# Turning the last two row tiles of a block by DMA instead of on TensorE, with two projections reordered, in a 32-head attention and SwiGLU kernel

## The chip, the cores and the metric

The kernel runs on one core of a Trainium2 chip. The metric is the time of one execution on the device, in microseconds (us); lower is better. All runs here are "fast": none is over 1.5% above the fastest of its kernel.

"PE" is TensorE (matmul), "PEld" its weight load, "DVE" VectorE, "ACT" ScalarE, "POOL" GpSimd, and "SP" or "SPq" the engine and queue that issue the DMAs followed here. "L410" is line 410 of the kernel. Times in the text count from the span's start.

## The reference

```python
# x: 1 x 2048 x 640; 32 heads, k and v caches 32 x 2048 x 192; all bf16
xn = layernorm(x)
q  = (xn @ wq) split into 32 heads of 192
s  = softmax(q @ k^T * 192**-0.5) @ v, heads joined, @ wo
g  = silu((silu(xn @ w1) * (xn @ w3)) @ w2)      # 640 -> 1536 -> 640
out = x + s * g
```

## The kernel before

x's 2048 rows are four blocks of 512 (`qb`), each of four row tiles of 128. Every projection needs the normalised block transposed (`xnT`: 640 features on partitions, rows along the free axis). A tile can be turned in two ways:

```python
def ln_turn(g, i2, copy):            # two tiles, on PE: ten 128x128 transposes into PSUM, then one copy
    pst = ps_st.tile([P, 2, DC, P], BF16, tag="st2", name="pst")
    for k in range(2):
        xn = xns.pop((g, 2 * i2 + k))
        for c in range(DC):
            nc.tensor.transpose(out=pst[:, k, c, :], in_=xn[:, c*P:(c+1)*P], identity=ident_bf[:])
    copy(out=xnT[...], in_=pst[:])

def ln_turn_dma(g, i):               # one tile, by a DMA transpose on the SP queue
    nc.sync.dma_start_transpose(out=xnT[:, :, q0:q0 + P], in_=xns.pop((g, i))[:])
```

`swap_halves(g)` then makes, with two DMAs, a copy `xnS` of the block with its partition halves exchanged; heads 1 to 31 need both. The work is a stream of steps. Step `n` of head `h` and block `qb` handles 256 keys (`p` counts them, eight steps to a block). `scores` is six matmuls into a PSUM tile of tag `st2`, then an exponential on ACT; `values` is sixteen matmuls. Scores run two steps ahead of values, and `st2` has two buffers, which projections and PE transposes share.

```python
for n, (h, qb, p) in enumerate(stream):
    if p == 0 and n > 0:
        project(h + 1, qb) ...       # next head's q of this block: 20 matmuls on xnT and xnS
    if h == 0 and qb == 0 and p == 3:
        project(1, 0)                # head 1's first projection
    if h == 0 and qb + 1 < NQB and p == (5 if qb == 0 else 4):
        project0(qb + 1)             # first head's q of the next block: 10 matmuls on xnT,
                                     # then casts (DVE, ACT) and three q copies (DVE)
    scores(n + 2)
    values(n)
    ...
    if h == 0:
        first_head(qb, p)            # layer norm of the blocks to come, on DVE, inside these steps
```

## Time and profile before

| | before |
|---|---|
| median of the first three runs | 1939.36 us (1938.64 to 1939.67) |
| profiled span | 1936.7 us |
| PE busy | 1927.1 us |
| granted clock | 1.0 |

From the page of the kernel before: the span, the busy time of PE, and the shares of the chain of work that ended last.

```profile
span 1936.7 us, 59668 instructions
PE 1927.1 (100%) x27273; PEld 1317.2 (68%) x27281; DVE 654.4 (34%) x997; ACT 1181.5 (61%) x1278; POOL 282.1 (15%) x501
PE 99%; DVE 0%; DMA 0%; ACT 0%; issue 0%
```

PE is busy for nearly the whole span, and it is also the chain that ended last. So the time is PE's work plus any hole in it, and an edit counts only if it takes PE work away or opens or closes a hole.

Next, a piece of that chain in order of time, before (start us, length us, what).

```profile
19.57 2.16 PE ps L424 x20
...
22.38 0.67 PE obank L516 x16
23.05 0.66 PE pst L354 x10
23.71 0.32 PE st L487
...
24.46 0.67 PE obank L516 x16
25.13 0.32 PE ps L410
...
25.50 1.89 PE ps L410 x8
27.39 0.32 PE st L487
```

Each piece starts where the last one ends. 19.57 is `project(1, 0)`, 23.05 the ten transposes, 25.13 `project0(1)`. The period from one value group to the next is 2.08 us across the transposes (22.38 to 24.46); an ordinary step takes 1.31.

The timeline of the same stretch, the normalisation of the two tiles, the SP queue and the copy that ends the PE turn (start us, busy us, engine, line, what, out<-in, count, idle time before and its releaser).

```profile
18.28 2.64 SPq L360 DMA_TRANSPOSE xnT<-xn  x2
...
20.66 0.80 DVE L346 TENSOR_SCALAR xn<-x_all,mv,rstd 128x640 bf16<-128x640 bf16 x2 [0.81 <-POOL rstd L327]
...
20.97 0.57 SPq L214 DMA_DIRECT2D x_all<-in_A_x_dram  x1
...
23.75 0.82 DVE L356 COPY xnT<-pst 128x1280 bf16<-128x1280 bf16 x1 [0.25 <-PE pst L354]
...
24.97 0.63 SPq L364 DMA_DIRECT2D xnS<-xnT  x1
```

The SP queue turns tiles 0 and 1 of block 1, then loads x's last block (640 KB, landed at 26.53), then swaps the halves of block 1 once the PE turn is copied out.

### The profile page before, as it was taken

Reading aid. Unit: us, or ns where it says so; the run is one execution under the profiler, and the core shown is the slowest. Engines: PE = TensorE matmul, PEld = TensorE weight load, DVE = VectorE, ACT = ScalarE, POOL = GpSimd, SP = SyncE. Lnnn points to the kernel's source line nnn. Section 1 sums busy time; section 2 is a strip of 40 time slices with the busy share of each in tenths; the row PEclk is TensorE's granted clock in tenths of the full one; section 3 lists DMA queues with packets and bytes.
Section 4 is the critical chain, followed back from the end, with each engine's and each line's share of the span. In section 5 each row is a group of like instructions: output and inputs, shape, how many; then the busy total and the mean of one; then the engine's idle time right before and its main releaser. Section 6 shows DMA issues by size and latency. Waiting matters only on the chain.

```text
span 1936.7 us, 59668 instructions
## 1 busy us (share of the span) xinstructions
PE 1927.1 (100%) x27273; PEld 1317.2 (68%) x27281; DVE 654.4 (34%) x997; ACT 1181.5 (61%) x1278; POOL 282.1 (15%) x501
## 2 busy tenths in 40 slices
PE   9999999999999999999999999999999999999998
PEld 6666666666666666666666666666666666577776
DVE  7333333333333333333333333333333334521111
ACT  6677676767676767776777777677767677210000
POOL 3111111111111111111111111111111110000000
PEclk9999999999999999999999999999999999999999
DMA  8643433323333434363434343434334220937772
GB/s 181 129 101 67 98 68 85 84 59 92 58 90 61 99 64 97 68 162 68 101 66 100 69 101 69 101 64 100 69 68 97 60 67 2 249 79 137 152 153 60
DMA packets 394643, 178.98 MB, mean 92 GB/s; under 512 B 341616, under 2 KB 382832, under 8 KB 394384
## 3 DMA queue, kind: packets, MB, share of 16 engines
q1 hardware_dynamic: 371136, 125.32, 31.5%
q0 software_dynamic: 19472, 45.71, 10.1%
q8 instruction: 215, 3.52, 0.8%
q10 hardware_dynamic: 3776, 4.06, 0.6%
q14 instruction: 44, 0.36, 0.1%
HBM read 52.82 MB, written 27.79 MB: 42 GB/s over the span
## 4 chain that ended last, share of the span: by engine, by line
PE 99%; DVE 0%; DMA 0%; ACT 0%; issue 0%
PE obank L516 35%; PE st L487 34%; PE ps L424 14%; PE ps_s L111 11%; PE ps_f L728 3%; PE ps_gu L702 1%; PE st L488 1%; PE ps L410 0%; DMA x_all<-in_A_x_dram 0%; DVE stats L316 0%; PE ps L391 0%; PE pst L354 0%; PE pk L271 0%; ACT pT L490 0%; DVE mv L317 0%
## 5 line engine op out<-in xcount | busy, mean ns | idle before, releaser
L490 ACT ACTIVATE pT<-st 128x1024 bf16<-128x1024 f32 x1024 | 1047.4, 1023 | 248.8 <-PE st L488 233.2
L516 PEld LDWEIGHTS <-pT 64*128 64x128 bf16 x16384 | 711.6, 94 | 242.0 <-ACT pT L490 0.2
L516 PE MATMUL obank<-vt,pT 64*128 64x193 bf16 x16384 | 849.6, 243 | 0.0
L487 PE MATMUL st<-qC,KW 64*128 64x512 bf16 x2046 | 605.6, 376 | 0.1
L525 DVE COPY osum<-obank 128x772 f32<-128x772 f32 x128 | 123.1, 962 | 786.9 <-PE obank L516 786.9
L488 PE MATMUL st<-qB,KW 64*128 64x512 bf16 x1024 | 385.0, 376 | 0.0
L487 PE MATMUL st<-qA,KW 64*128 64x512 bf16 x1022 | 384.3, 376 | 0.3 <-ACT pT L490 0.3
L488 PE MATMUL st<-qC,KW 64*128 64x512 bf16 x1022 | 384.3, 376 | 0.0
L488 PE MATMUL st<-qA,KW 64*128 64x512 bf16 x1022 | 384.3, 376 | 0.0
L487 PEld LDWEIGHTS <-KW 64*128 64x128 bf16 x3068 | 278.4, 94 | 153.3 <-issue 2.1
L424 PE MATMUL ps<-xnT,W 64*128 64x512 bf16 x1280 | 297.3, 376 | 0.0
L424 PE MATMUL ps<-xnS,W 64*128 64x512 bf16 x1280 | 296.2, 376 | 0.0
L488 PEld LDWEIGHTS <-KW 64*128 64x128 bf16 x3068 | 278.5, 94 | 0.8 <-issue 0.6
L377 POOL DMA_DIRECT2D qC<-qA x124 | 65.4, 528 | 1283.4 <-DVE rl_all L532 1268.5
L430 ACT CAST qB<-ps 128x512 bf16<-128x512 f32 x131 | 76.8, 586 | 228.2 <-PE ps L424 222.7
L111 PE MATMUL ps_s<-wo_sb,oT 128*128 128x384 bf16 (+3 forms) x1535 | 208.7, 299 | 0.1
L424 PEld LDWEIGHTS <-W 64*128 64x128 bf16 x2560 | 123.6, 94 | 120.7
L111 PEld LDWEIGHTS <-oT 128*128 128x128 bf16 x1536 | 148.4, 98 | 60.4
L526 DVE TENSOR_TENSOR osum<-osum,obank 128x772 f32<-128x772 f32 x128 | 122.7, 959 | 13.4
L533 DVE TENSOR_TENSOR ostage<-osum,rl_all 128x768 bf16<-128x768 f32 x128 | 122.6, 958 | 6.2 <-DMA o_scr<-ostage 1.9
L465 DVE SCALAR_TENSOR_TENSOR hT<-pt,qB 64x512 bf16<-64x512 bf16 x64 | 43.8, 684 | 197.6 <-ACT pt L464 197.6
L429 DVE CAST qA<-ps 128x512 bf16<-128x512 f32 x131 | 90.6, 692 | 25.3 <-PE ps L410 7.2
(84 smaller groups left out, 620.8 us busy)
## 6 DMA issues: line engine op xcount, KB each, us to landing
o_scr<-ostage SPq DMA_DIRECT2D x16, 1536.0 KB, 10.6
vt<-in_A_v_cache_dram SPq DMA_DIRECT2D x63, 384.0 KB, 5.9
qC<-qA POOLq DMA_DIRECT2D x248, 64.0 KB, 2.0
qC<-qB POOLq DMA_DIRECT2D x124, 64.0 KB, 2.3
wo_sb<-in_A_wo_dram POOLq DMA_DIRECT2D x1, 7680.0 KB, 37.8
W<-in_A_wq_dram POOLq DMA_DIRECT2D x32, 160.0 KB, 3.6
W<-in_B_w_dram POOLq DMA_DIRECT2D x32, 80.0 KB, 3.3
W<-in_A_wq_dram POOLq DMA_DIRECT2D x32, 80.0 KB, 2.9
```

The source lines that it names most:

```text
L111: nc.tensor.matmul(ps[:, 0:w], lhsT=oT[:, k, :], rhs=wo_sb[:, k, c0:c1], start=(k == 0), stop=(k == OC - 1))
L377: nc.gpsimd.dma_start(out=qC[0:64, half, :], in_=qAB[half][64:P, :])
L424: nc.tensor.matmul(ps[:, r * 512:(r + 1) * 512], lhsT=W[rows, j, :], rhs=xs[rows, j // 2, qs], start=(j == 0), stop=(j == 2 * DC - 1))
L429: a = nc.vector.tensor_copy(out=qAB[0][:], in_=ps[:, 0:512])
L430: b = nc.scalar.copy(out=qAB[1][:], in_=ps[:, 512:1024])
L487: nc.tensor.matmul(st2[:, 0:512], lhsT=ka, rhs=qa, start=r == 0 and nr == 3, stop=r == nr - 1)
L488: nc.tensor.matmul(st2[:, 512:1024], lhsT=kb, rhs=qb2, start=r == 0 and nr == 3, stop=r == nr - 1)
L490: nc.scalar.activation(out=pT2[:], in_=st2[:], func=ACT.Exp, scale=att_scale)
L516: nc.tensor.matmul(obanks[r][:, j * 256:j * 256 + DH + 1], lhsT=pT2[r * 64:(r + 1) * 64, t * 512 + j * P:t * 512 + (j + 1) * P], rhs=vt[r ...
L525: nc.vector.tensor_copy(out=osum[:], in_=ov[0])
L526: nc.vector.tensor_tensor(out=osum[:], in0=osum[:], in1=ov[1], op=ALU.add)
L533: nc.vector.tensor_tensor(out=ostage[:, qb * 4:qb * 4 + 4, hg * DH:(hg + 1) * DH], in0=osum[:, :, 0:DH], in1=rl.unsqueeze(2).to_broadcast( ...
```

## The change

The intent: take the last transposes off PE, give the DMAs one more step to land, and put head 1's first projection behind the first-head projection, so that PE has work while the new q is copied.

```diff
     def first_head(qb, p):
         if qb == 0 and p == 1:
-            ln_norm(1, 2, nc.vector)
-            ln_norm(1, 3, nc.vector)
+            for i in (2, 3):
+                ln_norm(1, i, nc.vector)
+                ln_turn_dma(1, i)
+            swap_halves(1)
         if qb == 0 and p == 3:
             ln_stats(2, 0)
-            ln_turn(1, 1, nc.vector.tensor_copy)
-            swap_halves(1)
@@ the loop over steps
-        if h == 0 and qb == 0 and p == 3:
+        if h == 0 and qb + 1 < NQB and p == (6 if qb == 0 else 4):
+            project0(qb + 1)
+        if h == 0 and qb == 0 and p == 6:
             project(1, 0)
-        if h == 0 and qb + 1 < NQB and p == (5 if qb == 0 else 4):
-            project0(qb + 1)
```

## The prediction

> **What bounds the kernel now.** TensorE: the page gives PE 1927.1 us busy of 1936.7 (100%), and the chain that ended last is 99% PE. From 15 us on, the chain of waits has no hole. A step of head 0 (scores 0.65 us of the chain, values 0.67) repeats every 1.31 us. So only PE work taken away, or a new hole in PE's stream, can matter. The change touches only the first 40 us.
>
> **What it removes.** Ten PE transposes of the last two row tiles of x's block 1: 0.66 us of the chain (23.05 to 23.71), and the score matmul behind them takes 0.32 instead of 0.21. The period between value groups is 2.08 us there (22.38 to 24.46), not 1.31: 0.77 us comes off the critical path. Their VectorE copy (0.82 us) goes too, off the path.
>
> **What it moves.** Head 1's first projection (2.16 us, at 19.57) goes behind block 1's first-head projection (2.2 us, at 25.13), itself a step later. This is neutral in PE work, and hides the q copies (1.5 us of VectorE, 27.44 to 28.96) that the next scores need.
>
> **What it adds.** Two DMA transposes, on which the first-head projection waits directly; it needs all 512 columns. Before, a projection and the transposes stood ahead of it on PE. Now three plain steps follow 19.57, so PE arrives at 19.57 + 3 x 1.31 = 23.5 us, earlier than the 25.1 of before although "a step later".
>
> VectorE ends the tiles' normalisation at 21.46. The SP queue first issues the load of x's last block (20.97 to 21.54), then the two transposes (1.2 to 1.3 us of issue each): at 21.6 and 22.9. The DMA view gives 2.6 to 5.1 us from issue to landing for such transposes, so the second lands at 25.5 at the earliest. The load ahead (640 KB) landed at 26.5. [...] So I expect landing near 27.7 (26 to 29.5). Estimated hole in PE: 27.7 - 23.5 = 4.2 us.
>
> **Balance.** +4.2 - 0.77 = +3.4 us. A possible extra: the granted clock fell to half 3.2 us after this trace's last matmul and rose 3.6 us after its first. If the hole trips this, some 3.5 us of matmuls run at half speed, +1.8 us; I give it one chance in three. Head 1's projection of block 1 follows the landing by about 7 us, and the half swap that it needs took 5.7 us from its issue: no second hole, narrowly.
>
> Predicted: 1943.0 us, 8 in 10 between 1940.3 and 1946.6: +0.2% on 1939.36. Faster by over 2%: 0.005; within 2%: 0.985; slower by over 2%: 0.01. Slower by any amount: 0.92.
>
> **What would show it.** In the timeline: no transposes near 23 us; three steps straight after 19.57; PE idle from 23.5 to about 27.7, released by the DMA of xnT, then the two projections back to back; later steps shifted by about 3.4 us with equal periods; PE clock below 1 near 26 to 31 us if the clock falls.
>
> **What would make it wrong.** Transposes that overtake the load (hole about 2 us, total +1.2); the clock falling, or a late half swap (+2 more); or transposes that land before 24 us: then 0.8 us faster.

## The result, and the profile after

| | before | after |
|---|---|---|
| median of six runs | 1938.84 us (1938.13 to 1939.67) | 1944.88 us (1943.27 to 1945.15) |
| profiled span | 1936.7 us | 1943.1 us |
| mean granted clock, profiled run | 1.0 | 0.998 |

The ratio is 1.0029 (95% interval 1.0016 to 1.0042): slower by 0.3%, the same by a margin of 2%. Ratios are the mean time of one kernel's fast runs over that of the other's of the same rounds, so they are not quite the ratios of the medians quoted here.

The page after, the same three lines:

```profile
span 1943.1 us, 59651 instructions
PE 1928.0 (99%) x27263; PEld 1315.4 (68%) x27271; DVE 653.6 (34%) x996; ACT 1180.2 (61%) x1278; POOL 282.4 (15%) x501
PE 98%; DMA 1%; DVE 0%; ACT 0%; SPq 0%; issue 0%
```

PE's busy time hardly moved (0.9 us more), but the span grew by 6.4, and a DMA now stands in the chain. The chain in order of time shows where:

```profile
22.84 5.72 DMA xnT<-xn
28.55 0.14 issue
28.69 0.58 PE ps L410
...
29.50 3.59 PE ps L410 x8
33.09 2.27 PE ps L424 x20
```

The second new transpose was issued at 22.84 and landed 5.72 us later, at 28.55. Only then could PE start `project0(1)`, which took from 28.69 to 33.09: 4.40 us, against 2.26 before (25.13 to 27.39). The timeline of the queue and of PE:

```profile
20.34 0.80 DVE L346 TENSOR_SCALAR xn<-x_all,mv,rstd 128x640 bf16<-128x640 bf16 x2 [0.81 <-POOL rstd L327]
...
20.66 0.57 SPq L214 DMA_DIRECT2D x_all<-in_A_x_dram  x1
...
21.33 3.54 SPq L360 DMA_TRANSPOSE xnT<-xn  x2
...
28.69 0.58 PE L410 MATMUL ps<-xnT,W 128*128 128x512 bf16 x1 [5.25 <-DMA xnT<-xn]
28.71 0.63 SPq L364 DMA_DIRECT2D xnS<-xnT  x1
...
29.50 3.59 PE L410 MATMUL ps<-xnT,W 128*128 128x512 bf16 x8 [0.22 <-issue]
```

PE stood idle for 5.25 us, released by the DMA of `xnT`. The transposes were issued right behind the load of x's last block. For the slow projection, the busy times of three stretches point to a reason of its own (stretch, length; then busy us and count of each engine; then the granted clock, the DMA share, GB/s):

```profile
22.69:26.10 3.41, 0.75 (x18) 0.52 (x13) 3.09 (x10) 1.54 (x2) 0.69 (x1) 1.00 1.11 205
26.10:32.93 6.83, 4.02 (x9) 1.31 (x10) 2.58 (x8) 0.00 (x0) 0.69 (x1) 0.50 0.69 165
32.93:36.00 3.07, 3.07 (x31) 1.44 (x32) 2.08 (x5) 1.17 (x2) 0.00 (x0) 1.00 0.63 116
```

From 26.10 to 32.93 the granted clock was 0.50, before and after it 1.00. That is 6.83 us, and PE worked through the last 4.24 of them (28.69 to 32.93) at half speed. That the clock is the reason is tested below.

The account of the profiled pair, from the start of step 3 (19.57 before, 19.26 after) to the end of step 7 (31.44 before, 37.98 after), is 11.87 us against 18.72, so +6.85:

| part | us |
|---|---|
| hole before `project0(1)` | +5.25 |
| `project0(1)` at half clock (4.40 - 2.26) | +2.14 |
| transposes and their step overhead gone | -0.77 |
| short gap at 21.07, before the values of step 4 | +0.21 |
| sum | +6.83 |

Step 4 needs the second half of v. After the change PE reaches that step 3.0 us earlier (21.28 against 24.30), and that load landed only at 21.24.

One thing of this execution is not the change's. Transfers that stand ahead of the changed ones landed 0.8 us later than in the profiled run before, though they were issued earlier: v's second half at 21.24 (before: 20.41), x's block 2 at 22.85 (22.01), tile 1 of block 1 at 25.66 (24.83). Another run with the same DMAs, e4_keep_busy below, was not late. The lines show where VectorE starts on block 2, which waits for that load, in the changed kernel and then in e4_keep_busy, and last that run's second transpose (issue, time to landing):

```profile
22.87 0.89 DVE L316 BATCH_NORM_STATS2 stats<-x_all 128x6 f32<-128x320 bf16 x2 [1.72 <-DMA x_all<-in_A_x_dram]
...
22.06 0.89 DVE L316 BATCH_NORM_STATS2 stats<-x_all 128x6 f32<-128x320 bf16 x2 [0.85 <-DMA x_all<-in_A_x_dram]
...
22.69 5.06 DMA xnT<-xn
```

### The profile page after: what moved, and what is told of

Read it like the earlier page. It is cut to its first block, busy times and chain, and to the rows that moved or that the text cites. A ratio compares the mean times of both kernels' runs of the same rounds, so it can differ in the third digit from the quotient of the medians.

```text
span 1943.1 us, 59651 instructions
## 1 busy us (share of the span) xinstructions
PE 1928.0 (99%) x27263; PEld 1315.4 (68%) x27271; DVE 653.6 (34%) x996; ACT 1180.2 (61%) x1278; POOL 282.4 (15%) x501
## 4 chain that ended last, share of the span: by engine, by line
PE 98%; DMA 1%; DVE 0%; ACT 0%; SPq 0%; issue 0%
PE obank L516 35%; PE st L487 33%; PE ps L424 14%; PE ps_s L111 11%; PE ps_f L728 3%; PE ps_gu L702 1%; DMA x_all<-in_A_x_dram 1%; PE st L488 1%; PE ps L410 0%; DMA xnT<-xn 0%; DVE stats L316 0%; ACT KW L277 0%; ACT xnT L356 0%; SPq L289 0%; PE pst L354 0%
```

## The experiments

All kernels ran with rounds of the kernel before on the same chip, and all passed the comparison with the reference. Three of the kernels compute a wrong q and passed it too, so the comparison does not see such an error.

| label | what it does | median us (range) | before, same rounds | ratio (95% interval) |
|---|---|---|---|---|
| e1_load_late | load behind the transposes | 1941.63 (1941.33 to 1941.82) | 1938.67 | 1.0012 (0.9996 to 1.0029) |
| e2_order_only | new order, PE turn | 1940.07 (1939.61 to 1941.15) | 1938.67 | 1.0004 (0.9987 to 1.0021) |
| e3_turn_only | old order, DMA turn | 1945.35 (1944.17 to 1946.02) | 1938.67 | 1.0032 (1.0015 to 1.0049) |
| e4_keep_busy | hole filled with thrown-away matmuls | 1942.16 (1942.02 to 1942.64) | 1938.67 | 1.0017 (1.0000 to 1.0033) |
| e5_no_wait | wrong: nothing to wait for | 1939.35 (1938.60 to 1939.50) | 1938.51 | 1.0003 (0.9989 to 1.0016) |
| e6_copy_first | e2, PSUM copy ahead of statistics | 1939.44 (1939.16 to 1940.05) | 1938.51 | 1.0004 (0.9991 to 1.0018) |
| e7_late_busy | e1 and e4 together | 1940.15 (1939.90 to 1940.78) | 1938.51 | 1.0008 (0.9993 to 1.0024) |
| e8_useful_work | e1, hole filled with needed work | 1938.92 (1938.73 to 1939.52) | 1938.51 | 1.0002 (0.9987 to 1.0017) |
| e9_no_wait_dve | e5, VectorE's statistics and norms later | 1938.99 (1938.03 to 1939.41) | 1938.59 | 1.0000 (0.9986 to 1.0014) |
| e10_useful_dve | e8, the same on VectorE | 1940.94 (1939.63 to 1942.91) | 1938.59 | 1.0009 (0.9995 to 1.0023) |
| e11_no_wait_stats | e5, only the statistics later | 1939.36 (1938.88 to 1941.95) | 1938.63 | 1.0006 (0.9992 to 1.0020) |

Most of these intervals hold 1. Where a few tenths matter, the verdict rests on the traces and not on the times, chiefly on the interval from the start of step 3 to the end of step 7, which is 11.87 us in the kernel before.

The first theory (A) was that the loss is the late landing of the transposes, and that the load ahead of them in the queue is much of the reason. The rivals were that the transposes set the landing themselves (B), that the new order costs time on its own (C), and, for the slow projection, the clock (D) or something else (E).

### The load behind the transposes

```diff
-        for g in range(3, NQB):
-            load_x(g)
@@ first_head, qb == 0 and p == 1
                 ln_turn_dma(1, i)
+            load_x(3)
             swap_halves(1)
```

> The changed kernel, with the load of x's last block issued behind the two new transposes instead of ahead of them. Theory A (the transposes land late[...]): the second transpose lands about 2 us earlier, near 26.5 instead of 28.55, the hole in PE shrinks from 5.25 to about 3 us, and the total falls by 2 us, by up to 4 if the clock then stays up. Rival B (the transposes themselves[...] set the landing): landing within 0.5 us of 28.5, hole at least 4.8 us, total unchanged at about 1944.9.

```profile
19.73 4.44 SPq L360 DMA_TRANSPOSE xnT<-xn  x3
...
24.22 0.57 SPq L214 DMA_DIRECT2D x_all<-in_A_x_dram  x1
...
26.20 0.59 PE L410 MATMUL ps<-xnT,W 128*128 128x512 bf16 x1 [2.67 <-DMA xnT<-xn]
...
27.00 3.13 PE L410 MATMUL ps<-xnT,W 128*128 128x512 bf16 x8 [0.22 <-issue]
```

The hole is 2.67 us instead of 5.25, the second transpose landed at 26.06 instead of 28.55, and the total fell by 3.3 us. So the load ahead of them was worth much of the landing, as theory A has it. How much is less sure than 2.5 us: block 2's load, ahead of both, already landed 0.67 us earlier here (22.18 instead of 22.85). Two kernels below that differ mainly in this load and whose block 2 landed at about the same time (e4_keep_busy 22.04, e7_late_busy 21.81) give 1.9 us (27.75 to 25.82), and 2.0 us of total. The rest fits B: even without the load, the second transpose took 3.6 us from its issue at 22.43, and tile 1, turned by DMA in every version (issued 19.73), landed only at 25.00. Why that one took 5.3 us was not found.

The clock fell here too, for 3.42 us. The parts add up again: 2.67 (hole) + 1.68 (projection 3.94 instead of 2.26) - 0.77 = 3.58, and the interval from step 3 to step 7 grew by 3.57 (19.59 to 35.03).

### The order alone, and the turn alone

The order-only kernel has the new order, and turns the tiles on PE at step 3 as before.

```diff
@@ after, first_head: without the two DMA turns and the swap of step 1, and back to
         if qb == 0 and p == 3:
             ln_stats(2, 0)
             ln_turn(1, 1, nc.vector.tensor_copy)
             swap_halves(1)
```

> Only the order of the change (first-head projection of block 1 one step later, head 1's first projection right behind it); the last two tiles are turned by PE as before. Theory A (all of the loss comes from waiting for the DMA): same as before within 0.4 us, about 1938.9, no PE hole over 0.3 us near 23 to 31 us. Rival C (the order itself costs, through PSUM buffers or the exposed q copies): 1 to 3 us slower than before, with holes around the two projections.

The median is 1.4 us slower than before, not within 0.4, so this expectation missed. The waits of its trace (engine, line, waited for: us in total, times, longest):

```profile
DVE stats L316 <- DMA x_all<-in_A_x_dram: 1.7, 1, 1.7
...
PE st L487 <- DVE xnT L356: 1.2, 1, 1.2
```

VectorE waited 1.7 us for the load of x's block 2, in front of the copy that empties the transposes' PSUM buffer. PE then waited 1.2 us for that copy, because the next scores need the buffer. In this trace the copy started only at 24.84, behind the statistics that ended at 24.68, though the transposes had ended at 23.07. Before the change, head 1's projection (2.16 us) stood in front of the transposes: the load landed at 22.01, and the transposes began only at 23.05. The profiled execution is the slowest of the four, because it reached step 3 1.5 us late; the interval leaves that out. The interval from step 3 to step 7 is 13.22 us (21.09 to 34.31), 1.35 over before, so this wait is nearly all of it.

The turn-only kernel has the DMA turn with the old order.

```diff
@@ after, the loop over steps: back to
         if h == 0 and qb == 0 and p == 3:
             project(1, 0)
         if h == 0 and qb + 1 < NQB and p == (5 if qb == 0 else 4):
             project0(qb + 1)
```

> Only the DMA turn of the change, in the old order (head 1's first projection at step 3, the first-head projection at step 5). Theory A: PE reaches the first-head projection near 24.1 us instead of 23.4 (2.16 us of projection ahead, one step less), the transposes land at 28.5 as in the changed kernel, hole about 4.5 us; total 0.7 us under the changed kernel if the clock falls as there, near 1944, or near 1942 if it stays up. Rival C (the order costs): near 1938 to 1940.

It is as slow as the whole change: the hole is 4.74 us (24.26 to 29.00), the projection 4.43 us at half clock, and the scores right behind it, partly at half clock, 1.24 us instead of 0.76. The interval grew by 6.63 us. So the turn by DMA carries the loss in either order, and the reorder did not buy the DMAs time: PE arrived at 23.44 with it and at 24.26 without it.

### The clock

```diff
@@ project0, after
+        if qb == 1:
+            for _ in range(20):      # thrown away: the real product starts the accumulation afresh
+                nc.tensor.matmul(ps[:, 0:512], lhsT=ident_bf[:], rhs=xnT[:, 0, 0:512], start=True, stop=True)
```

> The changed kernel, with 20 matmuls of 512 columns, thrown away, ahead of block 1's first-head projection, so that PE works through most of the hole (20 x 0.216 = 4.3 us). Theory D (2.1 us of the loss is that PE idled and its clock was halved for the projection): the clock stays at 1, the projection takes 2.25 instead of 4.40 us, the transposes land when they did, and the total falls by about 2.1 us to about 1942.8. Rival E (the projection is slow there for another reason, such as DMA traffic or its waits): projection still about 4.4 us, total unchanged or slower by up to 0.3 us.

```profile
23.20 4.49 PE L410 MATMUL ps<-xnT,ident_bf 128*128 128x512 bf16 x19
...
27.88 2.32 PE L413 MATMUL ps<-xnT,W 128*128 128x512 bf16 x10 [0.19 <-DMA xnT<-xn]
```

The line at 23.20 is the thrown-away work, the one at 27.88 the real projection (line 413 in this file). PE waits as long as before for the data, but does it busy: the clock stays at 1, the projection takes 2.32 us, and the total falls by 2.7 us. Theory D said 2.1; the rest fits the transposes' landing, 0.8 us earlier in this execution (27.75). E falls.

The two cures together:

```diff
@@ late-load kernel, project0
+        if qb == 1:
+            for _ in range(12):
+                nc.tensor.matmul(ps[:, 0:512], lhsT=ident_bf[:], rhs=xnT[:, 0, 0:512], start=True, stop=True)
```

> The late-load kernel with 12 thrown-away matmuls (2.6 us) ahead of block 1's first-head projection. If the losses add up (hole 2.7, clock 1.7, gain 0.77): the clock stays at 1, projection 2.3 us, total 1.6 us under the late-load kernel, about 1940.1. If a hole of 2.7 us had not cost clock there: unchanged at 1941.6.

1940.15 us against the 1940.1 expected, clock 1 in the trace. The losses add.

### Without the wait

The control reads block 0's columns in the two projections of block 1, which then wait for nothing. All other work stays, and q is wrong.

```diff
@@ project0, after
+        xb = 0 if qb == 1 else qb
-        qs = slice(qb * 512, (qb + 1) * 512)
+        qs = slice(xb * 512, (xb + 1) * 512)
@@ project, after
+        xb = 0 if (h, qb) == (1, 1) else qb
-        cast_pair(qAB, two_products(loads[h]["W"], slice(qb * 512, (qb + 1) * 512)))
+        cast_pair(qAB, two_products(loads[h]["W"], slice(xb * 512, (xb + 1) * 512)))
```

> The changed kernel, wrong on purpose: the two projections of x's block 1 that would wait for the turned tiles or for their swapped halves (first head's and head 1's) read block 0's columns instead, which have long been there. All other work stays. Theory A (the loss is the wait and what follows from it, and without it the change gains 0.77 us of PE): no PE hole from 19 to 32 us, clock at 1, step 3 to the end of step 7 in 11.1 us (before: 11.87), total 0.7 us under the kernel before, about 1938.0. Rival C (the order itself costs something): 1 us or more above that.

The hole and the low clock are gone, but the kernel is not under the one before: 1939.35 us, and the interval is 12.30 us, not 11.1. So C is partly right. The timeline of the control around the new q shows VectorE's cast and the first scores that need it:

```profile
27.96 0.69 DVE L430 CAST qA<-ps 128x512 bf16<-128x512 f32 x1
...
28.71 0.39 PE L489 MATMUL st<-qA,KW 64*128 64x512 bf16 x1 [0.59 <-DVE qA L430]
29.03 0.37 PE L490 MATMUL st<-qC,KW 64*128 64x512 bf16 x1
```

The projection ended at 25.85, yet the cast of its result started at 27.96: VectorE was still in the statistics and norms of block 2. The scores waited 0.59 us for it, and then ran one matmul at a time, each behind its q copy. In the changed kernel this backlog drains inside the 5.25 us hole and is not seen.

The same fault was tested in the order-only kernel, with the copy moved ahead of the statistics:

```diff
@@ order-only kernel, first_head, qb == 0 and p == 3
-            ln_stats(2, 0)
             ln_turn(1, 1, nc.vector.tensor_copy)
+            ln_stats(2, 0)
```

> The order-only kernel with one swap on VectorE: the copy that empties the transposes' PSUM buffer stands ahead of the statistics of x's block 2 instead of behind them. In the order-only kernel these statistics waited 1.7 us for their load and the copy behind them kept PE waiting 1.2 us. Theory F (that stall is the whole loss of the order-only kernel): no hole between steps 3 and 4, total about 1938.8, within 0.4 us of the kernel before. Rival C (the order costs elsewhere): stays near 1940.0.

PE no longer waits for the copy, but the median is 0.9 us over before, so theory F explains only part. The interval is 12.91 us: PE lost 0.27 us to a late normalisation before the transposes, and the scores behind the two projections took 1.28 us instead of 0.76, again behind the q copies.

Moving VectorE's block 2 work behind the casts settles it:

```diff
@@ no-wait kernel, first_head
-            i = p - 2 if qb == 0 else p - 1
+            i = {3: 1, 4: 2, 6: 3}.get(p, -1) if qb == 0 else p - 1      # last statistics: step 5 -> 6
-                if p == ((4, 7) if qb == 0 else (3, 5))[i2]:
+                if p == ((6, 7) if qb == 0 else (3, 5))[i2]:             # first norms: step 4 -> 6
```

> The no-wait kernel (wrong on purpose as before), with VectorE's statistics of the last tile of x's block 2 and the normalisation of its first two tiles moved from steps 4 and 5 behind the casts of step 6. Theory G (without the wait, the new order still cost 1.2 us because VectorE stood 2.1 us deep in block 2's statistics when the first-head projection ended, so the q copies and the scores behind them were late): the cast starts within 0.4 us of the projection's end, step 3 to the end of step 7 takes 11.1 to 11.4 us instead of 12.30, and the total falls by about 1 us, to about 1938.1, under the kernel before. Rival C (the order costs on PE itself): interval stays near 12.3 us.

```profile
25.97 0.68 DVE L430 CAST qA<-ps 128x512 bf16<-128x512 f32 x1
```

The busy times of its interval (columns as above):

```profile
19.58:30.68 11.10, 11.10 (x142) 6.75 (x140) 8.67 (x26) 6.79 (x9) 2.98 (x5) 1.00 0.91 171
```

The cast starts 0.19 us after the projection's end (25.78), and the interval is 11.10 us with PE busy in all of it: exactly 0.77 under before. So the gain is real, and with the wait and VectorE's backlog away it appears in full. Yet the total is 1938.99, not the 1938.1 expected. This trace has a new wait, "PE ps L411 <- DMA xnT<-xn" of 1.6 us: block 2's projection waits for its tiles. The first suspicion was that the moved norms turn these tiles later. With only the statistics moved:

```diff
@@ no-wait kernel, first_head
-            i = p - 2 if qb == 0 else p - 1
+            i = {3: 1, 4: 2, 6: 3}.get(p, -1) if qb == 0 else p - 1
```

> The no-wait kernel (wrong on purpose) with only the last statistics of x's block 2 moved behind the casts of step 6; the normalisation of block 2's first tiles stays where it was, so that their transposes are issued early enough. In the kernel that moved both, step 3 to the end of step 7 took 11.10 us as theory A and G had it, but block 2's transposes then came 1.6 us late for their projection. Expected here: 11.1 to 11.4 us for that interval and no hole over 0.3 us before block 2's projection; total 0.5 to 0.8 us under the kernel before. If the total is not under it, the gain of 0.77 us is lost at some further place.

The interval is 11.24 us, as expected, but the total (1939.36 us, 0.7 over before) is not, and block 2's projection still waits, by the view of the waits and by the timeline:

```profile
PE ps L411 <- DMA xnT<-xn: 1.9, 1, 1.9
...
40.27 2.32 PE L411 MATMUL ps<-xnT,W 128*128 128x512 bf16 x10 [1.95 <-DMA xnT<-xn]
```

The SP queue in its timeline:

```profile
...
28.11 0.63 SPq L364 DMA_DIRECT2D xnS<-xnT  x1
...
29.50 8.21 SPq L360 DMA_TRANSPOSE xnT<-xn  x4
```

The first half swap of block 1 waits on the SP queue for the new transposes, and was issued at 28.11 instead of 24.97. Block 2's transposes stand behind it on that queue. The last of them landed at 40.13 (before: 38.89), and PE gets to block 2's projection earlier (38.32 against 39.16). So the moved norms are not needed for the wait. In the kernel before, PE came only 0.14 us after it could have started there; the wait of 1.95 us is 0.84 of earlier arrival and 1.24 of later landing, less these 0.14. The late swap seems worth only some 0.4 of the landing: in e5_no_wait it was just as late (28.03), and the last transpose landed at 39.25. The rest came with the moved statistics, in a way that was not found. This is a third place where the gain goes: of 0.77 us gained in block 1, all but 0.14 needs block 2's transposes earlier as well. In the changed kernel the 6.8 us of delay hide it.

### Filling the hole with work that is needed

```diff
@@ late-load kernel, the loop over steps
+        if h == 0 and qb == 0 and p == 6:
+            project(1, 0)
         if h == 0 and qb + 1 < NQB and p == (6 if qb == 0 else 4):
             project0(qb + 1)
-        if h == 0 and qb == 0 and p == 6:
-            project(1, 0)
-        scores(n + 2)
-        values(n)
+        if n == 6: values(n); scores(n + 2)
+        else:      scores(n + 2); values(n)
```

> The late-load kernel with the hole filled by work that is needed anyway: head 1's first projection ahead of the first-head projection of block 1 (PE gets there at 25.7 instead of 23.5 us), and the value matmuls of step 6 between that projection and the next scores, to cover part of the q copies. Theory A: hole of about 0.4 us before the projection, about 0.4 to 0.9 us for the q copies behind it, clock at 1, total within 0.5 us of the kernel before (about 1938.9). If the clock falls even so: 1.7 us more.

1938.92 us, 0.4 over the kernel before in the same rounds, with the clock at 1. The hole is 0.71 us (25.52 to 26.23; the transposes landed at 26.10, and PE starts 0.13 later, as it does in the other runs), and the scores of step 8 and 9 together take 2.00 us (29.32 to 31.32) instead of 1.3, behind the q copies. The change's own order has the projection behind the wait; ahead of it, it shrinks the hole. This is the best correct version with the DMA turn, and it does not beat the kernel before.

The same with VectorE's block 2 work moved behind the casts:

```diff
@@ useful-work kernel, first_head: both lines of the no-wait kernel's first move
-            i = p - 2 if qb == 0 else p - 1
+            i = {3: 1, 4: 2, 6: 3}.get(p, -1) if qb == 0 else p - 1
-                if p == ((4, 7) if qb == 0 else (3, 5))[i2]:
+                if p == ((6, 7) if qb == 0 else (3, 5))[i2]:
```

> The useful-work kernel with the same move on VectorE: a correct kernel and the best candidate. By theory A and G: hole of 0.6 us before the first-head projection (transposes land near 26.1), 0.4 us before the scores of step 8 instead of about 0.7, clock at 1; step 3 to the end of step 7 in about 11.9 us, as in the kernel before (11.87); total equal to the kernel before within 0.3 us. A gain of over 0.5 us would show that the turn by DMA can pay at all.

This missed. VectorE's cast was no longer late, but the DMAs were: in the profiled execution, its slowest at 1942.91 us, the load of block 2 landed 0.8 us later than in the run above (the statistics start at 23.01 instead of 22.22), the transposes landed at 27.73, the hole was 2.13 us, and the clock fell once more. Block 2's projection waited another 0.60 us: its first transposes were issued at 35.21, against 27.63 in the run above. The other four runs took 1939.63 to 1940.99 us, still above all four of the useful-work kernel; they have no trace, and what slowed them stays open. The profiled execution shows how a kernel that lives on DMAs landing just in time inherits their spread.

## Why the prediction was right or wrong

It was right in time (1944.88 within 1940.3 to 1946.6, above the middle of 1943.0) and in its main mechanism, a wait for DMA transposes queued behind a load. The range of 6.3 us would have held the result with or without the clock's fall, so the hit says little about the clock. Point by point:

- **PE bounds, the change touches the first 40 us.** Right. Outside, steps keep their periods, and the span grew by what that stretch lost (6.85) less 0.45 us, of which 0.31 is that this execution started step 3 earlier.
- **0.77 us of PE comes off.** Right, and shown by itself in e9_no_wait_dve (11.10 us against 11.87).
- **PE arrives earlier, at 23.5, although "a step later".** Right: 23.44. Two things nearly cancelled: step 3 began 0.31 us early, and the wait for v cost 0.21.
- **The transposes land near 27.7, behind the load.** Right in kind, 0.9 us short: 28.55. The shortfall is about the 0.8 us by which block 2's load and other transfers ahead were already late in this execution. Where the same DMAs ran on time, in e4_keep_busy and e5_no_wait, block 2's load landed at 22.04 and 22.16 and the second transpose at 27.75 and 27.87, as forecast. That they land behind the load was the author's estimate. e1_load_late and e7_late_busy agree with it: there, moving the load out of the way brought the landing forward, by 2.5 us against the changed kernel and by 1.9 against e4_keep_busy.
- **The clock may fall, one chance in three, +1.8 us.** Right that the hole can trip it (0.50 in the changed kernel, 1.00 in e4_keep_busy), the chance too low. It fell in the profiled run and cost 2.14 us, and the mean clock was 0.998 in five of six runs and 0.999 in the sixth, which was the fastest (1943.27); 0.999 also occurs in runs of the kernel before, so whether it fell in the sixth is open. The clock stood at 0.50 for 3.42 us in e1_load_late, 3.41 in e10_useful_dve, and 6.83 after the change and in e3_turn_only.
- **The move is neutral and hides the q copies.** Wrong. It looked at the copies' own 1.5 us and not at what stood ahead of them in VectorE's queue. With the hole taken away, the scores waited for a cast that started 2.1 us late (e5_no_wait), and with the PE turn kept, the new order lost 1.2 us to the same queue (e2_order_only). The hole hid this.
- **No second hole.** Right for head 1's projection of block 1. But it did not look on to block 2: without the first hole, PE waits 1.9 us for block 2's transposes (e11_no_wait_stats), and the delayed swap seems to be only some 0.4 us of that.

The medians differ by 6.0 us where the balance said +3.4, or +5.2 with the clock. The terms that were mis-sized are the hole (5.25 instead of 4.2) and the chance of the clock's fall, whose cost (2.14 instead of 1.8) was nearly right.

What stays open: why a DMA transpose in this stretch takes up to 6.4 us (the first of the two new ones, 21.33 to 27.76). In the packets before the change, about a dozen packets of one transpose follow one after another, some 30 ns apart, from 23.50 to 23.84, while 15 packets of the load behind it, in flight for 1.6 to 1.9 us instead of 0.2, end together at 24.6. The reason was not shown: the trace does not name the DMA engines, and no experiment took the earlier loads away, since VectorE's statistics need them. In the same packets, one of 16 KB on the queue that the view calls "instruction" took 1.1 us (22.39 to 23.51 before, 23.28 to 24.38 after), and the transpose's late packets start as it ends (23.50 and 24.37). Whether the one has to do with the other was not shown; no run tested it.

## What to carry to other kernels

Before moving work from a busy engine to DMAs, write down two times: when the consumer will get there after the edit (removing or postponing work ahead of it makes it earlier), and when the data will land with everything that is queued ahead of it. When PE has to wait, give it needed work ahead of the wait rather than behind it, because here the clock also fell to 0.50, for 3.4 us with holes of 2.13 and 2.67 us, and for 6.8 with holes of 4.74 and 5.25. And when a stall disappears, look for what it hid: here the work queued on VectorE (1.2 us) and the wait for the next block's transposes (1.9 us) each took back more than the 0.77 us to be gained. And compare more than one trace before putting a size on a DMA's delay: the same transfers landed 0.8 us apart in two executions.

## What the traces show of the clock and of DMA transposes

- The granted clock fell to 0.50 in or right behind PE holes of 2.13 us (e10_useful_dve), 2.67 (e1_load_late), 4.74 (e3_turn_only) and 5.25 (after). In the 3.41 us before the fall PE had worked 1.28, 0.85, 0.12 and 0.75 us. It stayed at 1.00 through waits of 1.6 us (e9_no_wait_dve) and 1.95 us (e11_no_wait_stats); in the stretches of 3.41 us with these waits, or most of them, PE worked 1.87 and 1.93 us. That is six cases. Whether the length of the hole or the share of PE's work decides was not separated, and no limit is shown. The busy times of such stretches, late-load kernel, useful-work kernel with the VectorE move, and one without a fall:

```profile
22.68:26.09 3.41, 0.85 (x18) 0.61 (x14) 3.27 (x12) 1.54 (x2) 0.69 (x1) 1.00 1.20 121
26.09:29.51 3.42, 3.09 (x7) 1.20 (x9) 1.92 (x6) 0.00 (x0) 0.69 (x1) 0.50 0.91 281
```

```profile
24.52:27.93 3.41, 1.28 (x13) 0.51 (x10) 2.89 (x8) 0.62 (x2) 0.81 (x2) 1.00 0.97 168
27.93:31.34 3.41, 3.41 (x9) 1.19 (x10) 0.00 (x0) 0.00 (x0) 1.52 (x3) 0.50 0.88 242
```

```profile
38.34:41.75 3.41, 1.87 (x9) 0.91 (x10) 0.79 (x3) 0.41 (x1) 0.00 (x0) 1.00 0.44 91
```

- The DMA transpose of one row tile, 128x640 bf16 (160 KB), took 2.6 us from issue to landing in a quieter stretch (before, issued at 34.06; DMA share 0.45 until 36.70) and 6.4 and 5.7 us behind a 640 KB load (after, issued at 21.33 and 22.84; DMA share 0.86 from 23.44 to 28.69). Its issue alone held the SP queue for 1.2 to 2.7 us in these two traces.
